# Moving U behind x, zero matmuls ahead of the bands, and a new order of rounds 0 to 5 in a convolution and low-rank mixer kernel

## Chip, cores and metric

The kernel runs on one NeuronCore of a Trainium2 chip. The metric is the device time of one execution in microseconds (us). Before the change three runs gave 346.92, 348.03 and 348.5 us, median 348.03. One more execution was profiled: it took 345.57 us, and the program's own instructions span 343.8 us of it.

## What is computed

Inputs are x (8, 4224, 192), a small weight (8 heads, 7 taps), U (4224, 32), V (32, 4224), w_ch1 (192, 768) and w_ch2 (768, 192), all float32.

```python
w = softmax(weight)                    # 8 heads x 7 taps
y[b,s] = sum_k w[h,k] * x[b, s-6+k]    # causal convolution along s, by head of 24 channels
h = y^T @ U @ V                        # low-rank mixing along s, per batch element
u = y + h^T
out = u + relu(u @ w_ch1) @ w_ch2
```

## The kernel before

The sequence of each of the 8 batch elements is cut into 33 tiles of 128 rows; the 264 tiles of all batches form 33 groups of 8. The order of all work is written out by hand; every engine works its list strictly in that order.

**Start.** From the weight the kernel builds band matrices: softmax of the taps (L219 to L239, VectorE and ScalarE), a turn of the taps on TensorE (L246), seven small matmuls (L254), a product with a mask (L263) and copies into `band_sb` (L280 to L283). `keep_busy` (L213) puts matmuls of the identity, 512 columns each, ahead of and between these steps. Batch 0 is convolved by `conv_whole` (L402): each of four head pairs of each of five blocks of tiles (`blocks_0`) takes four matmuls with 128-row bands, and its result goes from PSUM to `y_sb` by ScalarE (L416) or VectorE (L418) in turn. U is loaded in float32 as 33 rows by the queues of ScalarE and SyncE (L112, L113) and turned on TensorE in four parts of 8 transposes (`turn_U`, L196): two ahead of the convolution, one behind each of its first two blocks. x goes in by GpSimd's queue (L88), cast to bf16 on the way; behind batch 0's five blocks stand V (L336), the halves of w_ch1 (L342), w_ch2 (L348) and batch 1 on that queue.

**Halo.** The convolution reaches six rows back into the tile before. Batch 0 does that with a second matmul. For later batches, `conv_parts` convolves only within the tile, and the first six rows of all tiles are made apart: `load_halo` (L101) loads the rows at the seams, `halo_parts` (steps `h` and `H`) multiplies them with `halo_band`, ScalarE evicts them (L477), one DMA writes them to DRAM (`hy_dr`, L487), and `put_halo` (step `s`, L493) reads them back into `y_sb`. Both DMAs are on SyncE's queue (SP).

**Rounds.** Round g = 0 to 32 does, for group g, the six chunks of the first channel matmul and relu (`m0` to `m5`, L645, evicted by ScalarE at L655 or VectorE at L657), and for group g-1 the second channel matmul in two halves (`P0`/`Q0`, `P1`/`Q1`, 24 matmuls each letter, L377), whose sum with u is formed by VectorE (L664) and written out by SP (L671). It also prepares group g+2: `x0`, `x1` form u (matmul L540, VectorE adds L552 and L560), and `t` turns it by a DMA on SP (L627) into `uT_sb`, which `m0` of round g+2 needs. `y0`, `y1` do the same for one more group. `T` is a turn on TensorE (L611, evicted at L619 and L620), `u` a turn of group 4 by DMA. `cN`/`dN` are the first and second half of a convolution unit; a batch has 8 units. `L` (`low_rank`, L506) is the product with U over all 33 tiles of a batch; its result, evicted by VectorE (L520, L523), is needed by every `x` or `y` step on tiles of that batch. Its first tile has no halo row from the DMA; the other 32 wait for `put_halo`.

Steps in two halves (`Halves`, L377) work on different 64-row parts of the same bank, so the second half waits for a GpSimd nop (L389) that waits for the first half. That nop stands on GpSimd's queue behind whatever loads the list puts there. PSUM has three rotating buffers `big` and one `ch`.

The lists of the rounds around the change, before:

```python
USUAL = "x0 m0 m1 P0 c0 m2 d0 c1 l0 Q0 d1 m3 s m4 L x1 t P1 m5 h Q1 H"
ORDERS = {
    0: "m0 y0 m1 y1 m2 m3 T m4 x0 m5 x1 t b",
    1: "m0 y0 m1 P0 c0 m2 d0 c1 Q0 d1 x0 m3 h m4 H y1 P1 c2 m5 d2 x1 t c3 c4 Q1 d3 d4",
    2: "m0 m1 P0 c0 m2 d0 c1 Q0 d1 m3 c2 m4 d2 s l0 P1 c3 m5 Q1 d3 L",
```

Functions that the diff touches:

Of the kernel before, what the change touches and what calls it, by code (L numbers as in the profile page):

```python
# [11 lines left out]
F32 = mybir.dt.float32  # L12
# [3 lines left out]
def kernel(  # L16
# [53 lines left out]
    def big(dtype=F32, pool=None):  # L70
        return (pool or big_ps).tile([P, 2, BK * 4 // mybir.dt.size(dtype)], dtype, name="big")
# [3 lines left out]

    x_tiles, hx_tiles, hx_bufs = {}, {}, []
    blocks_0 = [(0, 8), (8, 16), (16, 24), (24, 30), (30, NT)]
    assert blocks_0[0][1] >= GT
# [3 lines left out]
    def new_x(b):  # L82
        x_tiles[b] = xs.tile([P, NT + 1, D], BF16, name="x_sb")
        if b < 2:
            nc.vector.memset(x_tiles[b][:, 0, :].bitcast(mybir.dt.uint32), 0)
# [7 lines left out]
    def load_halo(b, s0=0, s1=HS):  # L93

        if s0 == 0 and b < 3:
            hx_bufs.append(cst.tile([P, HS, D], BF16, name=f"hx_sb{b % 2}"))
            nc.vector.memset(hx_bufs[-1][HJ * HP :, :, :], 0.0)
        hx = hx_bufs[(b - 1) % 2]
        for s in range(s0, s1):
            src = x[b, (s + 1) * P - HALO, :]  # L100
            nc.gpsimd.dma_start(  # L101
                out=hx[0 : HJ * HP, s, :],
                in_=bass.AP(src.tensor, src.offset, [[D, HP], [HS * P * D, HJ], [1, D]]),
            )
        hx_tiles[b] = hx

    w_sb = cst.tile([H, KC], F32, name="w_sb")
    nc.sync.dma_start(out=w_sb[:], in_=weight[:])

    U_rows = cst.tile([NT, P * R], F32, name="U_rows")  # L110
    U_dram = moe_U[:].rearrange("(j p) r -> j (p r)", p=P)
    nc.scalar.dma_start(out=U_rows[:, 0 : HB * R], in_=U_dram[:, 0 : HB * R])  # L112
    nc.sync.dma_start(out=U_rows[:, HB * R :], in_=U_dram[:, HB * R :])  # L113
    new_x(0)
# [10 lines left out]
    NA = -(-SP // KC)  # L125
    NCB = -(-(Q + HALO) // KC)
    ident = cst.tile([P, P], BF16, name="ident")
    nc.vector.memset(ident[:].bitcast(U32), 0)
# [37 lines left out]

    at_tap = cst.tile([KC, KC, NQ, Q], BF16, name="at_tap")
    load_x(0, *blocks_0[1])
    for s in blocks_0[2:]:
        load_x(0, *s)  # L170
# [8 lines left out]
    idle_ps = big(pool=ch_ps)  # L179
    ident_ap = ident[:]  # L180
    ident_4 = bass.AP(
        ident_ap.tensor, ident_ap.offset, [list(ident_ap.ap[0]), [0, BK // P], [1, P]]
    )


    ident_32 = cst.tile([NT, NT], F32, name="ident_32")
    nc.vector.tensor_copy(out=ident_32[:], in_=ident[0:NT, 0:NT])
    U_sb = cst.tile([P, R, NT], BF16, name="U_sb")
    UR = R // 4
    assert UR * NT <= BK  # L190

    def turn_U(n):

        ups = big()
        for r in range(UR):
            nc.tensor.transpose(  # L196
                out=ups[:, 0, r * NT : (r + 1) * NT],
                in_=U_rows[:].rearrange("j (p r) -> j r p", r=R)[:, n * UR + r, :],
                identity=ident_32[:],
            )  # L200
        return ups

    def evict_U(n, ups):
        src = ups[:, 0, 0 : UR * NT]
        dst = U_sb[:, n * UR : (n + 1) * UR, :].rearrange("p r j -> p (r j)")
        if n % 2 == 0:
            nc.scalar.activation(out=dst, in_=src, func=ACT.Copy)  # L207
        else:
            nc.vector.tensor_copy(out=dst, in_=src)

    def keep_busy(n):
        for _ in range(n):
            nc.tensor.matmul(  # L213
                out=idle_ps[:, 0, :], lhsT=ident[:], rhs=ident_4, start=True, stop=True
            )
# [12 lines left out]
    )  # L228
    nc.scalar.activation(
        out=halo_band[:].rearrange("p h c -> p (h c)"),  # L230
        in_=ident[:, 0:1].to_broadcast([P, H * P]),
        func=ACT.Copy,
        scale=0.0,
    )
    nc.vector.tensor_scalar_add(s_sb[:], s_sb[:], 1e-9)
# [5 lines left out]
    )  # L241
    for q in range(1, NQ):
        nc.vector.tensor_copy(out=in_band[q * Q : (q + 1) * Q], in_=in_band[0:Q])
    keep_busy(2)
    taps_ps = big(BF16)
    nc.tensor.transpose(out=taps_ps[0:KC, 0, 0:H], in_=tapsT[:], identity=ident[0:H, 0:H])  # L246
    taps = cst.tile([KC, H], BF16, name="taps")
    nc.vector.tensor_copy(out=taps[:], in_=taps_ps[0:KC, 0, 0:H])
    keep_busy(1)


    cps = big()
    for c in range(KC):
# [6 lines left out]
        )  # L260
    U_turned = [turn_U(0), turn_U(1)]
    local = cst.tile([P, H, NA * KC], BF16, name="local")
# [21 lines left out]

    for n, ups in enumerate(U_turned):
        evict_U(n, ups)

# [43 lines left out]

    def load_others():

        def load_V(c0, c1, quads):
            for q in range(quads):
                nc.gpsimd.dma_start(out=V_sb[q * R : (q + 1) * R, c0:c1], in_=moe_V[:, c0:c1])  # L336
            if quads < P // R:
                nc.sync.dma_start(out=V_sb[HB:, c0:c1], in_=V_sb[0:HB, c0:c1])

        load_V(0, V1, P // R)  # L340
        for h in range(2):
            nc.gpsimd.dma_start(  # L342
                out=W1_sb[h * HB : (h + 1) * HB],
                in_=moe_w_ch1[:].rearrange("(k r) m -> r k m", r=HB),
            )
        load_V(V1, 2 * V1, P // R)
        load_V(2 * V1, S, HB // R)
        nc.gpsimd.dma_start(out=W2_sb[:], in_=moe_w_ch2[:].rearrange("(m p) d -> p m d", p=P))  # L348
        new_x(1)
        for s in blocks:  # L350
            load_x(1, *s)

# [370 lines left out]
    for n, (s0, s1) in enumerate(blocks_0):  # L723
        for hh in range(0, H, 2):
            conv_whole(0, s0, s1, hh, hh // 2 % 2, ch_ps if n_conv % 4 == 3 else big_ps)
            n_conv += 1
        if n < 2:
            evict_U(2 + n, turn_U(2 + n))
        if n == 0:
            load_others()  # L730
            halo_masks()
    for s0, s1 in blocks_0:
        low_rank(0, s0, s1)
    straight_mix(0, [straight(0, k) for k in range(KB)])
    load_halo(1)
    new_x(2)
    for s in blocks:
        load_x(2, *s)
    load_halo(2)

    USUAL = "x0 m0 m1 P0 c0 m2 d0 c1 l0 Q0 d1 m3 s m4 L x1 t P1 m5 h Q1 H"
    ORDERS = {
        0: "m0 y0 m1 y1 m2 m3 T m4 x0 m5 x1 t b",
        1: "m0 y0 m1 P0 c0 m2 d0 c1 Q0 d1 x0 m3 h m4 H y1 P1 c2 m5 d2 x1 t c3 c4 Q1 d3 d4",
        2: "m0 m1 P0 c0 m2 d0 c1 Q0 d1 m3 c2 m4 d2 s l0 P1 c3 m5 Q1 d3 L",
        3: "m0 y0 m1 y1 u P0 c0 m2 d0 c1 l0 Q0 d1 x0 m3 m4 x1 t P1 c2 m5 d2 c3 h Q1 H d3",
        4: "x0 m0 m1 P0 c0 m2 d0 c1 l0 Q0 d1 m3 m4 x1 t P1 c2 m5 d2 s Q1",
        5: "x0 m0 m1 P0 c0 m2 d0 c1 l0 Q0 d1 m3 m4 x1 t P1 m5 h Q1 H L",  # L750
        NG - 1: "m0 m1 P0 m2 Q0 m3 m4 m5 W",
    }
    units = [(s0, s1, hh) for s0, s1 in blocks for hh in range(0, H, 2)]
    conv_by = {g: [] for g in range(NG)}
    steps = {g: {} for g in range(NG)}
    for nb in range(1, B):
        last = (nb * NT) // GT - AHEAD - 1
        if nb == 1:
            last, shares = 2, {1: 5, 2: 3}
        elif nb == 2:  # L760
            shares = {2: 1, 3: 4, 4: 3}
        else:
            shares = {g: 2 for g in range(last - 4, last)}
        left = list(units)
# [4 lines left out]
        assert not left  # L769
        at = 3 if nb == 2 else min(shares)  # L770
        steps[at]["h"], steps[at]["H"] = halo_parts(nb)
        steps[max(shares)]["s"] = lambda nb=nb: put_halo(nb)
        steps[last]["L"] = lambda nb=nb: low_rank(nb, 0, NT)
        if nb + 2 < B:


            b, g = nb + 2, max(shares) + (nb > 1)
            for n in range(2):
                steps[g + n]["l0"] = lambda b=b, n=n: (
                    new_x(b) if n == 0 else None,  # L780
                    load_x(b, *blocks[n]),
                )
            steps[g + 2]["l0"] = lambda b=b: load_halo(b)
    for g in range(NG):
# [3 lines left out]
        for m in range(MC):  # L788
            on_act = m not in ((2, 4, 5) if len(conv_by[g]) > 2 and g > 1 else (2, 4))
            if g == 0:  # L790
                on_act = m != 4
            by[f"m{m}"] = lambda g=g, m=m, on_act=on_act: h1_chunk(g, m, on_act)
# [6 lines left out]
        if g != 2 and g + AHEAD < NG:  # L799
            for n in range(2):  # L800
                by[f"x{n}"] = lambda g=g, n=n: mix_quad(g + AHEAD, n * QT)
            by["t"] = lambda g=g: turn_by_dma(g + AHEAD)
        more = {0: 1, 1: 0, 3: 4}
        if g in more:
            for n in range(2):
                by[f"y{n}"] = lambda g=g, n=n: mix_quad(more[g], n * QT)
    steps[0]["T"] = lambda: turn(1, True)
    steps[3]["u"] = lambda: turn_by_dma(4)
    steps[0]["b"] = build_halo_band
    for g in range(NG):  # L810
# [38 lines left out]
```

## Time and profile before

| what | value |
|---|---|
| median of 3 runs | 348.03 us |
| profiled execution | 345.57 us, span 343.8 us, mean granted TensorE clock 0.997 |
| TensorE (PE) busy | 324.3 us, 94% of the span |
| VectorE (DVE), ScalarE (ACT) busy | 229.9 us (67%), 190.4 us (55%) |
| GpSimd (POOL) busy | 48.6 us |
| chain that ended last | PE 70%, DMA 6%, DVE 2% |
| m chunks, L645 | 1188 matmuls, 153.5 us busy |
| W2 and convolution halves, L377 | 3024 matmuls with W_sb, 146.9 us; 224 with band_sb, 34.3 us |
| convolution of batch 0, L402 | 80 matmuls, 10.9 us |

A line of the profile's timeline has start, duration, engine, line, operation, output<-inputs, shape, count, and in brackets the idle time before it with what ended it. Busy times of matmuls overlap, since a matmul is counted until its modelled end; for a pace the starts of neighbouring groups are compared. A table of windows gives busy time of each engine in each stretch, the granted TensorE clock (PEclk), the DMA engines' share and GB/s.

### The profile page before, as it was taken

How to read it: one execution, taken by the hardware profiler on the slowest of the kernel's cores; microseconds unless marked ns; L12 is line 12 of the kernel's file. 1: busy time of each engine (PE TensorE's matmuls, PEld its weight loads, DVE VectorE, ACT ScalarE, POOL GpSimd, SP SyncE). 2: the span in 40 equal slices, each digit the busy share in tenths (PEclk: the TensorE clock that was granted, in tenths of full speed). 3: DMA queues.
4: the chain of work that ended last, by engine and by line, in shares of the span. 5: the costliest groups of instructions: out<-in, count | busy, mean ns of one | idle time of the engine just before them, and what ended most of it. 6: DMA issues, size and time to landing. Idle time of an engine off the chain costs nothing.

```text
span 343.8 us, 11906 instructions
## 1 busy us (share of the span) xinstructions
PE 324.3 (94%) x5319; PEld 243.3 (71%) x5319; DVE 229.9 (67%) x334; ACT 190.4 (55%) x222; POOL 48.6 (14%) x77
## 2 busy tenths in 40 slices
PE   4988888989999999989999999999999999999994
PEld 2874665667677777767777777777777777777774
DVE  5358646957676676657666786667666777777553
ACT  5247564565566656656566665665766444444550
POOL 8485101111012011201012011200000000000000
PEclk9999999999999999999999999999999999999998
DMA  8999997997999669995999699976444644455524
GB/s 129 197 175 193 183 206 119 173 205 165 139 176 236 158 119 210 169 210 148 161 206 236 111 165 193 221 179 143 115 129 136 148 141 139 145 158 157 144 94 139
DMA packets 124064, 56.48 MB, mean 164 GB/s; under 512 B 89008, under 2 KB 123520, under 8 KB 123904
## 3 DMA queue, kind: packets, MB, share of 16 engines
q1 hardware_dynamic: 84160, 39.73, 49.0%
q0 software_dynamic: 39808, 15.70, 39.8%
q8 instruction: 42, 0.69, 0.9%
q10 hardware_dynamic: 44, 0.27, 0.3%
q14 instruction: 10, 0.08, 0.1%
HBM read 32.45 MB, written 26.47 MB: 171 GB/s over the span
## 4 chain that ended last, share of the span: by engine, by line
PE 70%; DMA 6%; DVE 2%; issue 0%; ACT 0%; ACTq 0%
PE big L377 34%; PE big L645 30%; DMA uT_sb<-u_sb 6%; PE big L540 2%; PE big L712 2%; PE big L506 2%; DVE o_sb L664 2%; DVE tt_sb L523 0%; DVE tf_sb L520 0%; ACT hy_sb L477 0%; ACTq L655 0%
## 5 line engine op out<-in xcount | busy, mean ns | idle before, releaser
L655 ACT ACTIVATE rl_sb<-big 128x1024 bf16<-128x1024 f32 x130 | 129.4, 1022 | 87.1 <-PE big L645 84.6
L645 PE MATMUL big<-uT_sb,W_sb 64*128 64x512 bf16 x1188 | 153.5, 376 | 4.3 <-DMA uT_sb<-u_sb 1.4
L377 PE MATMUL big<-W_sb,rl_sb 64*128 64x192 bf16 x3024 | 146.9, 243 | 0.0
L377 PEld LDWEIGHTS <-rl_sb 64*128 64x128 bf16 x3024 | 130.6, 94 | 16.3 <-issue 0.2
L657 DVE TENSOR_SCALAR rl_sb<-big 128x1024 bf16<-128x1024 f32 x68 | 83.3, 1225 | 67.3 <-PE big L645 66.2
L645 PEld LDWEIGHTS <-W_sb 64*128 64x128 bf16 x1188 | 62.7, 94 | 45.3 <-issue 6.2
L664 DVE TENSOR_TENSOR o_sb<-big,u_sb 128x768 f32<-128x768 f32 (+1 forms) x68 | 63.4, 933 | 25.8 <-PE big L377 21.1
L416 ACT ACTIVATE y_sb<-big 128x816 bf16<-128x816 f32 (+4 forms) x66 | 50.7, 771 | 46.1 <-PE big L377 37.3
L552 DVE TENSOR_TENSOR u_sb<-y_sb,big 128x384 bf16<-128x384 bf16 x128 | 64.7, 547 | 1.2 <-PE big L540 1.0
L88 POOL DMA_DIRECT2D x_sb<-in_x_dram x19 | 21.9, 1158 | 118.5 <-PE big L377 117.1
L377 PE MATMUL big<-x_sb,band_sb 64*128 64x408 bf16 (+1 forms) x224 | 34.3, 328 | 1.3 <-ACT rl_sb L655 0.7
L540 PE MATMUL big<-tt_sb,V_sb 64*128 64x192 bf16 x264 | 23.3, 243 | 1.5 <-DVE tt_sb L523 1.0
L101 POOL DMA_DIRECT2D hx_sb<-in_x_dram x28 | 16.0, 578 | 47.0 <-PE big L377 41.9
L540 PEld LDWEIGHTS <-V_sb 64*128 64x128 bf16 x264 | 13.0, 94 | 9.9 <-issue 2.1
L377 PEld LDWEIGHTS <-band_sb 64*128 64x128 bf16 x224 | 12.8, 94 | 7.7 <-issue 1.5
L402 PE MATMUL big<-x_sb,band_sb 128*128 128x192 bf16 (+2 forms) x80 | 10.9, 328 | 0.9 <-DMA x_sb<-in_x_dram 0.9
L402 PEld LDWEIGHTS <-band_sb 128*128 128x128 bf16 x80 | 9.6, 142 | 1.5 <-ACT U_sb L207 1.0
L418 DVE CAST y_sb<-big 128x384 bf16<-128x384 f32 (+2 forms) x10 | 4.8, 488 | 6.8 <-PE big L402 6.8
L506 PEld LDWEIGHTS <-U_sb 128*32 128x32 bf16 x264 | 6.3, 138 | 3.8 <-issue 3.6
L506 PE MATMUL big<-y_sb,U_sb 128*32 128x192 bf16 x264 | 7.8, 252 | 1.2 <-DMA y_sb<-hy_dr 0.8
L477 ACT ACTIVATE hy_sb<-big 48x384 bf16<-48x384 f32 x14 | 6.0, 478 | 4.1 <-PE big L377 4.1
L712 PE MATMUL big<-W_sb,rl_sb 128*128 128x192 bf16 x72 | 6.3, 246 | 1.0 <-DVE o_sb L664 1.0
(66 smaller groups left out, 68.1 us busy)
## 6 DMA issues: line engine op xcount, KB each, us to landing
out_dram<-o_sb SPq DMA_DIRECT2D x65, 384.0 KB, 6.1
x_sb<-in_x_dram POOLq DMA_DIRECT2D x7, 816.0 KB, 11.1
x_sb<-in_x_dram POOLq DMA_DIRECT2D x7, 768.0 KB, 11.4
x_sb<-in_x_dram POOLq DMA_DIRECT2D x3, 384.0 KB, 7.6
hx_sb<-in_x_dram POOLq DMA_DIRECT2D x28, 36.0 KB, 5.8
W_sb<-in_moe_w_ch_dram POOLq DMA_DIRECT2D x3, 288.0 KB, 6.4
V_sb<-in_moe_V_dram POOLq DMA_DIRECT2D x8, 64.0 KB, 6.6
hy_dr<-hy_sb SPq DMA_DIRECT2D x7, 72.0 KB
```

The lines of the kernel that those rows point to most:

```text
L88: nc.gpsimd.dma_start(out=x_tiles[b][:, 1 + s0 : 1 + s1, :], in_=x[b, s0 * P : s1 * P, :].rearrange("(j p) d -> p j d", p=P),)
L101: nc.gpsimd.dma_start(out=hx[0 : HJ * HP, s, :], in_=bass.AP(src.tensor, src.offset, [[D, HP], [HS * P * D, HJ], [1, D]]),)
L377: mm = nc.tensor.matmul(out=out_, lhsT=lhsT[rows], rhs=rhs[rows], start=not second and n == 0, stop=bool(second) and n == N - 1,)
L402: nc.tensor.matmul(out=cps[:, q, 0:n], lhsT=band_sb[:, hh + q, w, :], rhs=x_tiles[b][:, 1 + s0 - w : 1 + s1 - w, hc], start=(w == 0), stop ...
L416: nc.scalar.activation(out=dst, in_=src, func=ACT.Copy)
L506: nc.tensor.matmul(out=tps[q * R : (q + 1) * R, 0, 0:D], lhsT=U_sb[:, :, j], rhs=y_sb[:, j, :], start=(j < n), stop=(j >= NT - n),)
L540: nc.tensor.matmul(out=ups[:, t, i * D : (i + 1) * D], lhsT=V_sb[rows, j * P : (j + 1) * P], rhs=tt_tiles[b][rows, :], start=True, stop=True,)
L552: nc.vector.tensor_tensor(out=dst, in0=y_tiles[b][:, j : j + 2, :].rearrange("p t (k r) -> p t k r", r=HB), in1=add, op=ALU.add,)
L645: nc.tensor.matmul(out=h1[:, q, :], lhsT=W1_sb[rows, k, m * P : (m + 1) * P], rhs=ut[rows, k, :, :], start=(k == 0), stop=(k == KB - 1),)
L655: nc.scalar.activation(out=rl, in_=src, func=ACT.Relu)
L657: nc.vector.tensor_scalar_max(out=rl, in0=src, scalar1=0.0)
L664: nc.vector.tensor_tensor(out=o_sb[:, 0:w, :].rearrange("p t (k r) -> p t k r", r=HB), in0=ch.rearrange("p t (k r) -> p t k r", r=HB), in1 ...
```

## The change

U is loaded in bf16 by GpSimd's queue, behind the second block of x, and turned in two parts of 16 transposes behind the second block of the convolution. Batch 0 has four blocks (8, 11, 9, 5 tiles) in place of five. The matmuls of `keep_busy` take a tile of zeros, which VectorE clears first, in place of the identity that GpSimd makes, and there are 8 + 1 + 5 of them in place of 2 + 1. V goes in by four loads for each column block, with no copy by SP; w_ch1 goes in by halves of its columns; batch 1's two halves, the halo masks and batch 1's halo rows follow on GpSimd's queue. The last block's part of batch 0's low-rank product comes behind the two straight turns of group 0. Group 2 is turned on TensorE in round 1 in place of a DMA in round 0. Batch 1 is convolved in rounds 1 and 2 by 4 + 4 units (5 + 3 before), batch 2 in rounds 3 and 4 by 4 + 4 (1 + 4 + 3 in rounds 2 to 4 before). Batch 1's halo steps `h`, `H` go from round 1 to round 2, and its `L` from the end of round 2 to round 3, behind `m0`. Later loads of x stand at the start of a round.

```diff
-    blocks_0 = [(0, 8), (8, 16), (16, 24), (24, 30), (30, NT)]
+    blocks_0 = [(0, 8), (8, 19), (19, 28), (28, NT)]
...
-    U_rows = cst.tile([NT, P * R], F32, name="U_rows")
-    nc.scalar.dma_start(out=U_rows[:, 0 : HB * R], in_=U_dram[:, 0 : HB * R])
-    nc.sync.dma_start(out=U_rows[:, HB * R :], in_=U_dram[:, HB * R :])
...
+    idle_sb = cst.tile([P, BK], BF16, name="idle_sb")
+    nc.vector.memset(idle_sb[:].bitcast(U32), 0)
...
+    U_rows = cst.tile([NT, P * R], BF16, name="U_rows")
     load_x(0, *blocks_0[1])
+    for c in (slice(0, HB * R), slice(HB * R, P * R)):
+        nc.gpsimd.dma_start(out=U_rows[:, c], in_=U_dram[:, c])
...
-                out=idle_ps[:, 0, :], lhsT=ident[:], rhs=ident_4, start=True, stop=True
+                out=idle_ps[:, 0, :], lhsT=idle_sb[:, 0:P], rhs=idle_sb[:], start=True, stop=True
...
-    for q in range(1, NQ):
-        nc.vector.tensor_copy(out=in_band[q * Q : (q + 1) * Q], in_=in_band[0:Q])
-    keep_busy(2)
+    keep_busy(8)
...
-    U_turned = [turn_U(0), turn_U(1)]
+    keep_busy(5)
...
+    load_V(0, V1)
+    load_W1(slice(0, M4 // 2))
+    load_V(V1, 2 * V1)
+    load_W1(slice(M4 // 2, M4))
+    load_V(2 * V1, 3 * V1)
+    nc.gpsimd.dma_start(out=W2_sb[:], in_=moe_w_ch2[:].rearrange("(m p) d -> p m d", p=P))
+    new_x(1)
+    load_x(1, *blocks[0])
+    load_V(3 * V1, S)
+    load_x(1, *blocks[1])
+    halo_masks()
+    load_halo(1)
...
-        if n < 2:
-            evict_U(2 + n, turn_U(2 + n))
-        if n == 0:
-            load_others()
-            halo_masks()
-    for s0, s1 in blocks_0:
+        if n == 1:
+            turn_U(0)
+            turn_U(1)
+    for s0, s1 in blocks_0[:-1]:
         low_rank(0, s0, s1)
-    straight_mix(0, [straight(0, k) for k in range(KB)])
-    load_halo(1)
-    new_x(2)
-    for s in blocks:
-        load_x(2, *s)
-    load_halo(2)
+    yts = [straight(0, k) for k in range(KB)]
+    low_rank(0, *blocks_0[-1])
+    straight_mix(0, yts)
...
+    USUAL = "l x0 m0 m1 P0 c0 m2 d0 c1 Q0 d1 m3 s m4 L x1 t P1 m5 h Q1 H"
     ORDERS = {
+        0: "m0 m1 y0 m2 y1 m3 T m4 x0 m5 x1",
+        1: "l m0 m1 m2 T y0 P0 c0 m3 d0 c1 Q0 d1 c2 c3 d2 d3 y1 P1 x0 m4 m5 x1 t Q1 b",
+        2: "l m0 m1 c0 P0 c1 d0 c2 d1 Q0 d2 m2 c3 h d3 P1 H m3 s m4 m5 Q1",
+        3: "l m0 L c0 P0 y0 d0 c1 Q0 y1 u d1 m1 m2 m3 x0 P1 c2 c3 d2 x1 t d3 Q1 m4 m5",
+        4: "l c0 c1 d0 d1 m0 P0 c2 c3 d2 d3 x0 Q0 m1 h m2 H P1 m3 s m4 m5 x1 t Q1",
+        5: "l x0 m0 m1 P0 c0 m2 d0 c1 Q0 d1 m3 m4 x1 t P1 L m5 Q1",
...
+    loads = {
+        1: lambda: (new_x(2), load_x(2, *blocks[0])),
+        2: lambda: (load_x(2, *blocks[1]), load_halo(2)),
+        3: lambda: (new_x(3), load_x(3, *blocks[0])),
+        4: lambda: load_x(3, *blocks[1]),
+        5: lambda: load_halo(3),
+    }
...
+    for g in range(2):
+        steps[g]["T"] = lambda g=g: turn(g + 1, True)
```

## Prediction

> **What bounds the kernel now.** First the table of windows, by stage (columns: busy us of PE, PEld, DVE, ACT, POOL, then PEclk, DMA share, GB/s):
>
> ```profile
> 0.00:25.00 25.00, 19.35 (x188) 16.01 (x189) 12.15 (x37) 10.20 (x21) 17.42 (x36) 1.00 1.17 167
> 25.00:57.00 32.00, 28.18 (x403) 18.03 (x401) 20.42 (x31) 20.32 (x25) 8.67 (x12) 1.00 1.26 178
> 57.00:93.00 36.00, 32.70 (x571) 24.16 (x572) 26.06 (x39) 19.38 (x24) 4.77 (x6) 1.00 1.06 167
> 93.00:320.00 227.00, 225.05 (x3887) 170.05 (x3885) 160.57 (x218) 132.89 (x147) 17.77 (x23) 1.00 0.84 165
> ```
>
> From 93 us on TensorE is full: 2 us idle in 227. There every step has a fixed price, read from the starts of neighbouring groups: an m chunk 0.648 us, a P or Q 0.99, a unit's half 0.162 or 0.172, an x, y, h or H 0.165, L 0.86. The change alters almost nothing there; what it can win lies ahead of 93 us. Charging each step its price, TensorE waits 6.6 us between 24.8 us (round 0) and `L` of batch 1 (56.55), 1.1 at that `L`, and 4.3 from there to 92.5.
>
> Then the timeline of TensorE at the start, and the end for comparison:
>
> ```profile
> 8.99 2.72 PE L402 MATMUL big<-x_sb,band_sb 128*128 128x192 bf16 x16 [0.89 <-DMA x_sb<-in_x_dram]
> 11.64 1.09 PE L196 MATMUL big<-ident,U_rows 33*128 33x33 f32 x8
> 12.67 2.74 PE L402 MATMUL big<-x_sb,band_sb 128*128 128x192 bf16 x16
> 15.34 1.09 PE L196 MATMUL big<-ident,U_rows 33*128 33x33 f32 x8
> 16.37 5.45 PE L402 MATMUL big<-x_sb,band_sb 128*128 128x192 bf16 x48
> ...
> 335.91 4.12 PE L712 MATMUL big<-W_sb,rl_sb 128*128 128x192 bf16 x48 [1.05 <-DVE o_sb L664]
> ```
>
> The last 48 of batch 0 stream 16 x (192+144+72) = 6528 columns in 5.45 us, 1.2 a ns; L712 streams 9216 in 4.12, 2.2 a ns. So the convolution of batch 0 ran at half the clock, though the windows print 1.00: the trace has no clock record ahead of 21.19 us, and at that moment the spacing of 72-column matmuls falls from 60 to 33 ns. Half clock cost about 5 us.
>
> Last, what the clock does when TensorE rests, behind the last matmul (ended 340.03):
>
> ```profile
> 340.10:342.00 1.90, 0.00 (x0) 0.00 (x0) 0.32 (x1) 0.00 (x0) 0.00 (x0) 1.00 1.06 354
> 342.10:343.70 1.60, 0.00 (x0) 0.00 (x0) 0.00 (x0) 0.00 (x0) 0.00 (x0) 0.50 0.09 29
> ```
>
> It falls to half 2 us after the last matmul. The two changes of clock, 21.19 and 342.04, lie 94 x 3.413 us apart; so I take windows of about 3.4 us: one 41% busy closed the clock, and those cut by turns of U (66 to 70% convolution) did not open it.
>
> **Part 1, the start.** Before, x landed at 8.86, 11.01, 13.06, 14.67 and 15.43 (the waits of GpSimd's later loads show it): 1200 KB in 6.57 us, 183 KB a us. TensorE at half clock was slower than that, at twice the pace x is. U's 528 KB leave the first microseconds: the first block's packets came 2.6 us after issue where a later load's (54.59) took 2; I take 8.4. Then 528 KB of x, to 11.3; U, 264 KB at the 205 a us of V's loads, to 12.6; 432 KB, to 15.0; 240 KB, to 16.3. Zero matmuls: they start at 1.4, behind a clear of 0.2 us, where the identity kept them until 2.84; eight at 0.427 us (512 columns at 1.2 a ns) last until 4.8, 0.2 past `tapsT` (4.63); the taps copy now stands ahead of 0.98 us of `in_band` copies, and the bands are done at 7.6 as before, under x's 8.4. With the five more TensorE works from 1.4 to at most 7.7, long enough for a whole window nearly always, so I take the full clock. The last block then needs 16 x 55 ns, until 17.3, where before it ended at 21.8. Its eviction (0.7, as `low_rank` shares that PSUM tile), `low_rank` 0.76, two straight turns 0.72, the last `low_rank` 0.14, copy of `part` 0.56, `straight_mix` and its eviction 1.4: first m chunk at 21.6, before 24.8. **-3.2 us.** At half clock throughout: 11.3 + 3.5 + U's turns 1.4 + 2.9 + 1.6 = 20.7, **-0.5**. If x came at 205 a us and U beside it, -4.2.
>
> **Part 2, rounds 0 to 2 and m0 of round 3.** Work: round 0 six m, four x or y, a turn of 12 x 56 ns: 5.2. Round 1 six m, four P or Q, eight unit halves, four x or y, the added turn 0.67, b: 10.7. Round 2 six m, four P or Q, eight halves, h, H: 9.5. Then m0: 0.65. Sum 26.1, against 25.2 before to its `L`. Waits: with three buffers, evictions of 0.97 (ACT m), 1.23 (DVE m), 1.0 (DVE add of an x step), 0.8 (unit), I went through the lists in order and get 4.3 against 6.6: DVE has no 0.8 of halo clears and 0.55 of `halo_band` in round 0, ACT's five m and a turn set its length. TensorE reaches `L` at 21.6 + 26.1 + 4.3 = 52.0; before, 56.55.
>
> Costed at nothing: V's 16 loads and w_ch1's four halves (about 0.5 us of GpSimd each) push batch 1's first half from 30.85 to 31-33; c0 is at 34.8. Without that cover GpSimd's nops queue behind two halo issues and one load of x (0.58+0.58+1.25), up to 2.4. The DMA turn of group 2 (384 KB, 12 us to land) is gone; nobody waited for it.
>
> **Part 3, the wait at L.** Here I see the price. Before, batch 1's halo left ScalarE at 42.3 and `L` came 14 us later; now only m3, m4, m5, Q1 and m0 lie between `H` and `L`: 3 x 0.648 + 0.99 + 0.65 = 3.6 us. The route is long (SP's timeline, then TensorE's):
>
> ```profile
> 42.32 0.33 SPq L487 DMA_DIRECT2D hy_dr<-hy_sb  x1
> 54.52 0.29 SPq L493 DMA_DIRECT2D y_sb<-hy_dr  x1
> ...
> 56.55 0.29 PE L506 MATMUL big<-y_sb,U_sb 128*32 128x192 bf16 x1
> 57.63 0.89 PE L506 MATMUL big<-y_sb,U_sb 128*32 128x192 bf16 x32 [0.79 <-DMA y_sb<-hy_dr]
> ```
>
> Before, SP held the read back until batch 1's last eviction (54.5), so the first leg was covered. By the landing marks, `hy_dr` takes 7.8, 6.1, 6.1, 7.4, 6.7, 6.3 us where x is loading and SP's queue has transfers ahead of it, and 2.55 for the seventh, alone; the read back 3.1 to 5.7. New: H ends at 48.4, eviction 0.2 + 0.86 plus backlog, issue at 49.7. Ahead of it in SP's queue stand group 3's turn (about 41.6) and two outputs, beside x of batch 2 until about 50, then batch 3's first half: landing at 54.9, inside the loaded rows' range less a little; read back 3.3: `L` goes on at 58.2, 6.2 us after it was reached (bounds 55.3 and 63). Everything on TensorE stands behind it: c0, P0, y0; DVE and ACT run dry; SP's outputs stand behind the read back.
>
> 6.2 us contain a whole window, so the clock closes. Half clock until the first full window, 3.4 to 6.8 us, mean 4.5: half is lost, 2.2, less 0.5 of waits on evictions that vanish: +1.7 (bounds 0 and 3.4).
>
> A rule against this change: the Trainium skill (TensorE: Matmul & The Clock Gate, Why this matters for your kernels) asks for no TensorE gap over about 3 us. The rows above price it: half clock for one to two windows, 1.7 to 3.4, so a sum of -0.2 to +1.5.
>
> **Part 4, behind L.** The work left is before's less m0 (0.65), plus one unit of batch 2 (0.34): -0.3. Waits: 4.3 before (0.6 for `tt`, 1.0 and 0.4 at h and H of round 3, 0.8 for group 4's uT, 1.3 at L of batch 2). Now `tt` has c0 and P0 over it, batch 2's `L` has m5 and Q1, group 4's uT lands 4.2 to 8 after issue with 5.6 of work over it: I take 2.1. Gain -2.2.
>
> From round 6 on the order is before's with h one round later and loads moved; two rounds (17 us) remain between H and `L`. Taken as 0, bounds -1 to +1 (one uT wait of 1.4 at 147 us may go or come).
>
> **Sum.** `L` goes on at 58.2 against 57.63: +0.6; clock +1.7; behind -0.3 - 2.2: -0.2 us. 345.57 - 0.2 = 345.4 in the profiled frame (1.8 of it around the span). The median is 2.46 higher: **347.8 us, no change that can be measured** (this kernel's runs tell 0.5%, 1.7 us, from none).
>
> **Rivals.**
> (a) *The halo's route is short.* If SP's queue is empty when `hy_dr` is issued: 2.55 + 3.07, `L` goes on at 55.3, 3.3 us late; the clock closes about half the time (+0.8). -2.3 + 0.8 - 2.5 = -4.0: **344.0**. For it: uncontended rows exist, and group 2's turn is gone from the queue. Against: x of batches 2 and 3 loads just then. 0.35.
> (b) *The zero matmuls don't hold the clock* (the change doesn't do what it says; slower). They open it too late, or the waits for x (8.4, then 9.8 to 11.3, each leaving a window about half busy) close it again. Then the start gains 0.5, not 3.2, and all behind moves by 2.7: -0.2 + 2.7: **350.5**. It decides if a window about half busy closes the gate: one 41% busy did, one 82% busy (21.2 to 24.6) did not. 0.2. By the Trainium skill (TensorE: Matmul & The Clock Gate, Part 1) only a wholly idle window closes it, and (b) would fall; the row at 342 us, where the window still had 1.4 us of matmuls, speaks against that, so (b) stays.
> (c) *The route is longest*: 7.8 + 3.8, `L` at 61.3, and the clock stays half for two windows: +3.7 + 3.4 - 2.5 = +4.6: **352.6**. 0.1.
> Forecast 0.35.
>
> **Numbers.** The forecast's own range: a start of -4.2 and the steady rounds' -1 give 345.8, the clock's 3.4 gives 349.5. The range of 8 in 10 takes in (a) and (b) with their bounds: 341.5 to 352.5. Faster by over 0.5%: (a), 0.35; within: 0.35; slower: (b) and (c), 0.3.
>
> **What would show it.** Spacing of L402's 192-column matmuls, 82 ns (160 in (b)); first m chunk at 21.6; L402's waits for x_sb; a wait of L506 on `y_sb` of 6 us near 52 with granted clock 0.50 behind it; no wait over 1 us at c0 of round 1. I'm wrong if L506 doesn't wait, or if GpSimd's nops wait behind its loads.

## The result and the profile after

| | before | after |
|---|---|---|
| median, 20 runs each, us | 346.0 (343.02 to 350.83) | 350.75 (347.9 to 353.12) |
| ratio of the times | | 1.0148, 95% 1.0114 to 1.0182 |
| profiled execution, span, us | 345.57, 343.8 | 353.12, 351.4 |
| mean granted clock of the profiled execution | 0.997 | 0.973 |

The change makes the kernel 1.5% slower, 5.1 us, where -0.2 us was forecast. That 350.75 lies inside the stated range of 341.5 to 352.5 is luck: the prediction started from a median of 348.03, which over 20 runs is 346.0, and 1.0148 times 348.03 is 353.2, outside. The profiled execution of after is the slowest of its 20: nine of them had a granted clock of 0.973 to 0.979 and took 350.03 to 353.12 us, five had 0.985 to 0.989 and took 347.9 to 350.66.

Line numbers are those of each run's own kernel, so a step's line differs from that of before. The table of windows of after, by the same stages (busy us of PE, PEld, DVE, ACT, POOL; PEclk; DMA share; GB/s):

```profile
0.00:24.80 24.80, 19.16 (x183) 12.89 (x184) 11.44 (x35) 9.64 (x18) 17.77 (x34) 0.86 1.04 135
24.80:56.30 31.50, 29.06 (x417) 18.76 (x417) 19.93 (x29) 21.97 (x26) 13.23 (x24) 1.00 1.36 174
56.30:63.80 7.50, 0.50 (x11) 0.34 (x13) 0.06 (x1) 1.02 (x1) 0.00 (x0) 0.69 1.27 215
63.80:69.30 5.50, 5.50 (x80) 4.51 (x74) 2.14 (x6) 0.85 (x1) 0.00 (x0) 0.50 0.00 0
```

The start takes as long as before, 24.8 us. Its clock of 0.86 can't be set against the 1.00 of before, whose trace has no record ahead of 21.19 us. Then come a hole of 7 us and 5.5 us at half clock behind it. TensorE's timeline of after, at the start and at the hole:

```profile
7.24 1.78 PE L398 MATMUL big<-x_sb,band_sb 128*128 128x192 bf16 x16 [0.59 <-ACT band_sb L268]
11.42 3.57 PE L398 MATMUL big<-x_sb,band_sb 128*128 128x264 bf16 x16 [2.40 <-DMA x_sb<-in_x_dram]
14.93 2.19 PE L191 MATMUL big<-ident,U_rows 33*128 33x33 bf16 x32
17.05 3.67 PE L398 MATMUL big<-x_sb,band_sb 128*128 128x216 bf16 x32
...
24.77 0.39 PE L641 MATMUL big<-uT_sb,W_sb 64*128 64x512 bf16 x2 [0.26 <-ACT uT_sb L596]
...
56.28 0.29 PE L502 MATMUL big<-y_sb,U_sb 128*32 128x192 bf16 x1
63.57 1.51 PE L502 MATMUL big<-y_sb,U_sb 128*32 128x192 bf16 x32 [7.00 <-DMA y_sb<-hy_dr]
```

The first 16 matmuls of L398 ran at full clock (1.78 us for 16 x 192 columns), the next 16, at 11.42, at half (3.57 us for 16 x 264, 1.2 columns a ns). Why shows in windows laid on the clock's changes, which fall 3.41 us apart:

```profile
4.50:7.90 3.40, 2.70 (x21) 1.21 (x20) 2.70 (x10) 1.56 (x3) 3.40 (x6) 1.00 1.43 161
7.90:11.30 3.40, 1.12 (x14) 0.89 (x11) 1.19 (x3) 1.35 (x3) 1.21 (x3) 1.00 1.31 169
11.32:14.72 3.40, 3.30 (x16) 2.25 (x16) 1.15 (x2) 0.61 (x1) 1.74 (x3) 0.50 1.50 186
14.73:18.13 3.40, 3.40 (x46) 3.18 (x45) 1.20 (x3) 1.35 (x3) 1.51 (x4) 1.00 1.16 180
18.15:21.50 3.35, 2.89 (x32) 2.64 (x33) 1.52 (x4) 1.66 (x4) 3.35 (x7) 0.50 0.96 133
```

A window 33% busy (the wait for x) is followed by one at half clock. The one from 14.73 is full by the table, but 2.19 us of it are the turns of U (L191); it too is followed by half clock. So windows less than about half full close the gate, which is rival (b)'s mechanism, and turns don't fill them, which is in none of the rivals. The Trainium skill (TensorE: Matmul & The Clock Gate, Part 1) puts the fall to half rate behind a window of idleness; the window here was 33% busy and one of e11, shown below, 40%, so the measured share decides. By the Trainium skill (TensorE: Matmul & The Clock Gate, Part 4: PE-mode transpose) transposes don't count as busy in the same way; the window from 14.73 agrees.

SP's timeline of after has the halo's route:

```profile
45.23 4.13 SPq L623 DMA_TRANSPOSE uT_sb<-u_sb  x1
49.41 1.99 SPq L667 DMA_DIRECT2D out_dram<-o_sb  x2
53.35 0.57 SPq L483 DMA_DIRECT2D hy_dr<-hy_sb  x1
58.56 0.32 SPq L489 DMA_DIRECT2D y_sb<-hy_dr  x1
```

The write to DRAM landed at 58.54, right behind the two outs queued ahead of it (56.94 and 58.35); the read back took until 63.53. A load of x, half of batch 3, was in flight beside both (issued at 52.94, landed at 63.32).

### The profile page after: what moved, and what is told of

The parts are those of the page before. It is cut to its first block, busy times and chain, and to the rows that moved or that the text cites. A ratio compares the mean times of both kernels' runs of the same rounds, so it can differ in the third digit from the quotient of the medians.

```text
span 351.4 us, 11913 instructions
## 1 busy us (share of the span) xinstructions
PE 327.6 (93%) x5326; PEld 239.2 (68%) x5326; DVE 224.5 (64%) x327; ACT 194.5 (55%) x224; POOL 53.4 (15%) x86
## 4 chain that ended last, share of the span: by engine, by line
PE 75%; DMA 16%; DVE 3%; ACT 2%; issue 1%; POOL 0%; POOLq 0%; ACTq 0%
PE big L373 35%; PE big L641 30%; DMA uT_sb<-u_sb 11%; PE big L536 2%; PE big L502 2%; DMA x_sb<-in_x_dram 2%; PE big L398 2%; PE big L708 2%; DVE o_sb L660 1%; DMA hy_dr<-hy_sb 1%; DMA y_sb<-hy_dr 1%; ACT rl_sb L651 1%; ACT y_sb L412 1%; PE big L191 1%; DVE u_sb L548 1%
## 5 line engine op out<-in xcount | busy, mean ns | idle before, releaser
L651 ACT ACTIVATE rl_sb<-big 128x1024 bf16<-128x1024 f32 x134 | 133.6, 1022 | 88.8 <-PE big L641 87.6
L641 PE MATMUL big<-uT_sb,W_sb 64*128 64x512 bf16 x1188 | 151.4, 376 | 4.9 <-DMA uT_sb<-u_sb 1.8
L653 DVE TENSOR_SCALAR rl_sb<-big 128x1024 bf16<-128x1024 f32 x64 | 78.4, 1225 | 63.0 <-PE big L641 61.7
L641 PEld LDWEIGHTS <-W_sb 64*128 64x128 bf16 x1188 | 59.7, 94 | 49.1 <-issue 8.3
L412 ACT ACTIVATE y_sb<-big 128x816 bf16<-128x816 f32 (+5 forms) x64 | 49.9, 790 | 47.1 <-PE big L373 39.3
L89 POOL DMA_DIRECT2D x_sb<-in_x_dram x18 | 21.6, 1203 | 129.0 <-PE big L641 52.0
L502 PEld LDWEIGHTS <-U_sb 128*32 128x32 bf16 x264 | 7.0, 141 | 10.5 <-issue 10.4
L398 PE MATMUL big<-x_sb,band_sb 128*128 128x192 bf16 (+3 forms) x64 | 8.9, 316 | 3.1 <-DMA x_sb<-in_x_dram 2.4
L398 PEld LDWEIGHTS <-band_sb 128*128 128x128 bf16 x64 | 6.8, 126 | 5.1 <-DMA x_sb<-in_x_dram 2.6
L327 POOL DMA_DIRECT2D V_sb<-in_moe_V_dram x16 | 8.1, 527 | 5.0 <-DMA x_sb<-in_x_dram 5.0
L516 DVE COPY tf_sb<-big 64x192 f32<-64x192 f32 x8 | 2.9, 359 | 9.0 <-PE big L502 8.8
L414 DVE CAST y_sb<-big 128x384 bf16<-128x384 f32 (+3 forms) x8 | 4.6, 570 | 5.6 <-PE big L398 5.4
```

The source lines that it names most:

```text
L89: nc.gpsimd.dma_start(out=x_tiles[b][:, 1 + s0 : 1 + s1, :], in_=x[b, s0 * P : s1 * P, :].rearrange("(j p) d -> p j d", p=P),)
L398: nc.tensor.matmul(out=cps[:, q, 0:n], lhsT=band_sb[:, hh + q, w, :], rhs=x_tiles[b][:, 1 + s0 - w : 1 + s1 - w, hc], start=(w == 0), stop ...
L502: nc.tensor.matmul(out=tps[q * R : (q + 1) * R, 0, 0:D], lhsT=U_sb[:, :, j], rhs=y_sb[:, j, :], start=(j < n), stop=(j >= NT - n),)
L641: nc.tensor.matmul(out=h1[:, q, :], lhsT=W1_sb[rows, k, m * P : (m + 1) * P], rhs=ut[rows, k, :, :], start=(k == 0), stop=(k == KB - 1),)
L651: nc.scalar.activation(out=rl, in_=src, func=ACT.Relu)
L653: nc.vector.tensor_scalar_max(out=rl, in0=src, scalar1=0.0)
```

## The experiments

Theory A: batch 1's halo comes back too late for the earlier `L`; the wait and the half clock behind it eat the gain. Theory B: the start lost it, since the gate closes on the waits for x and on the turns. Rivals: the new order of rounds, or the contention with loads of x, is what costs. A zero matmul is one of `idle_sb`, 512 columns; `hold(n)` issues n of them. Edits are to the changed kernel unless another is named; ratios are to the kernel before.

**e1: no wait for the halo.** Batch 1's halo rows are made and written to DRAM but not added to y.

```diff
-        steps[max(shares)]["s"] = lambda nb=nb: put_halo(nb)
+        if nb > 1: steps[max(shares)]["s"] = lambda nb=nb: put_halo(nb)
```

> The halo rows of batch 1 are not read back into y (the step s of batch 1 is left out), so L has no DMA to wait for; six rows of each tile of batch 1 then lack their halo. Theory A (the loss is the wait at L and the clock that closes in it): the wait of 7.0 us goes, the clock stays at 1.00 from the first rounds on, 5.5 us of half clock behind L go (2.7 us of time). Time 9 to 10 us below the changed kernel, ratio to the kernel before 0.985 to 0.990. Theory B (the loss is at the start, where the clock closed twice; at L the time would come back in other waits, of evictions or of the turns by DMA): 0 to 3 us below, ratio 1.006 to 1.015.

Ratio 0.9879 (0.9829 to 0.9929), 2.7% or 9.3 us below after. TensorE's timeline has no hole:

```profile
55.97 0.96 PE L502 MATMUL big<-y_sb,U_sb 128*32 128x192 bf16 x33
56.87 0.35 PE L373 MATMUL big<-x_sb,band_sb 64*128 64x408 bf16 x2
```

Theory A is shown: without the wait the change beats the kernel before by 4.2 us. The first m came at 24.34 all the same, so the start is a loss of its own. The gain without the wait also answers the rival that the new order of rounds is what costs: on balance it isn't.

**e2 and e11: zero matmuls in the hole,** 33 and 20, between round 3's `m0` and its `L`.

```diff
-        3: "l m0 L c0 P0 ...",
+        3: "l m0 z L c0 P0 ...",
+    steps[3]["z"] = lambda: hold(33)   # e11: hold(20)
```

> 33 matmuls of zeros, 512 columns each (7.1 us at 0.216), stand between m0 and L of round 3, so TensorE works while the halo is on its way. Theory A with the clock as its second half: the wait at L falls to under 1 us, its time is filled and not won, the clock stays open behind L, and 2.7 us are won: ratio about 1.007. If the half clock behind L costs nothing (evictions would bound those steps anyway): ratio 1.015 as before. If zeros don't keep the gate open: clock 0.50 behind L and 1.015.

> The changed kernel with 20 zero matmuls (some 4.3 us at full clock) between the m of round 3 and its L, so that they end before the halo's return lands, while the 33 of the earlier run ran past it. The route of the halo is as it was, the wait at L should fall from 7.0 to about 2.7 us. If the price of the closed clock is the 2.7 us by which the time behind L differs between the changed kernel and the version without the wait, and the filled window stays open, the run is 2.7 us shorter than the changed kernel: ratio 1.005 to 1.008. If the window closes all the same, on the 2.7 us that are left idle, the ratio stays at 1.013 to 1.017.

e2: 1.0104 (1.0048 to 1.0161), between the two expectations. The clock was full behind `L`, from which 279.7 us remained to the last matmul against 283.2 in after, but the zeros ran 2.1 us past the landing: in its profile group 3's turned tile came 2.8 us late ahead of them, and the clock was half from 56.70 to 60.12, while they ran. e11: 1.0065 (1.0023 to 1.0107), the number that the first theory gave, but not its mechanism: the windows of e11 show that the 2 us left idle closed the gate all the same, for one window (three in after).

```profile
53.61:57.01 3.40, 3.35 (x16) 1.54 (x16) 0.00 (x0) 1.02 (x1) 0.00 (x0) 1.00 1.58 205
57.02:60.42 3.40, 1.36 (x15) 0.54 (x17) 0.00 (x0) 0.00 (x0) 0.00 (x0) 1.00 1.02 198
60.43:63.83 3.40, 3.40 (x60) 2.77 (x55) 1.06 (x3) 0.00 (x0) 0.00 (x0) 0.50 0.01 3
```

From `L` on to the last matmul e11 took 282.4 us, 0.8 less than after. Where the rest of its 2.9 us comes from its one profile can't tell: that run's start was also at full clock throughout (first m 21.15).

**e3: the halo a round earlier.** `b`, `h`, `H` in round 1, `s` right behind `d3` in round 2.

```diff
-        1: "... y0 P0 c0 ... y1 P1 x0 m4 m5 x1 t Q1 b",
-        2: "... Q0 d2 m2 c3 h d3 P1 H m3 s m4 m5 Q1",
+        1: "... y0 b P0 c0 ... y1 P1 h x0 m4 H m5 x1 t Q1",
+        2: "... Q0 d2 c3 m2 d3 s P1 m3 m4 m5 Q1",
...
-            last, shares, at = 3, {1: 4, 2: 4}, 2
+            last, shares, at = 3, {1: 4, 2: 4}, 1
```

> The halo steps h and H of batch 1 go into round 1 (its band b ahead of them), and s stands right behind the last unit of round 2. Nothing else moves. Theory A: the write of the halo rows is issued near 43 instead of 53, ahead of group 3's turn in SP's queue, and lands before the last unit is evicted near 52; the read back lands 3 to 5 us later, at 55 to 57, with L reached at 56: wait at L 0 to 1.5 us, clock open behind it, 7 to 10 us below the changed kernel, ratio 0.986 to 0.995. Theory B: 0 to 3 us below. A third way: h waits for its rows (landed 39.3) or its nop behind a load, and round 1 grows by 1 to 3 us: ratio 0.993 to 1.003.

1.0009 (0.9966 to 1.0051), 4.8 us less than after, but above the 0.986 to 0.995 of theory A. SP's timeline and TensorE's show why not all of it:

```profile
42.38 0.35 SPq L483 DMA_DIRECT2D hy_dr<-hy_sb  x1
43.58 3.50 SPq L623 DMA_TRANSPOSE uT_sb<-u_sb  x1
47.13 1.95 SPq L667 DMA_DIRECT2D out_dram<-o_sb  x2
50.17 2.06 SPq L489 DMA_DIRECT2D y_sb<-hy_dr  x1
```

```profile
54.40 0.82 PE L641 MATMUL big<-uT_sb,W_sb 64*128 64x512 bf16 x6 [1.94 <-DMA uT_sb<-u_sb]
55.15 0.30 PE L502 MATMUL big<-y_sb,U_sb 128*32 128x192 bf16 x1
58.84 1.50 PE L502 MATMUL big<-y_sb,U_sb 128*32 128x192 bf16 x32 [3.39 <-DMA y_sb<-hy_dr]
```

The read back is issued 8.4 us earlier than in after (58.56), but behind group 3's turn (landed 54.36) and two outs (to 57.95): 8.6 us, to 58.80. So `m0` and `L` waited 5.3 us in all, and the clock was half from 55.39 to 62.21.

**e9: group 3 turned on TensorE in round 2,** not by DMA; the halo where the change put it. **e6: both,** e3 and this.

```diff
-        1: "... x1 t Q1 b",
-        2: "l m0 m1 c0 ...",
+        1: "... x1 Q1 b",
+        2: "l m0 m1 T c0 ...",   # e6: T behind P1, the halo steps as in e3
...
-            if g > 0: by["t"] = lambda g=g: turn_by_dma(g + AHEAD)
+            if g > 1: by["t"] = lambda g=g: turn_by_dma(g + AHEAD)
...
-    for g in range(2):
+    for g in range(3):
         steps[g]["T"] = lambda g=g: turn(g + 1, True)
```

> The changed kernel with only group 3's turn moved from SP's queue to TensorE, in round 2. The halo steps stay where the change put them. In the changed kernel turn, two outputs, halo write and read back landed at 55.5, 56.9, 58.4, 58.5 and 63.5. If the queue ahead sets the halo's route: the write lands 3 us earlier, the read back too, the wait at L falls from 7.0 to 3 to 5 us, ratio 1.003 to 1.010. If the route has its own length (2.6 us and 3.1 us are the shortest rows, 5 and 5 the ones here): wait 6 to 7 us, ratio 1.013 to 1.017.

> As e3_early_halo (batch 1's h and H in round 1, s behind the last unit), and group 3 is turned on TensorE in round 2 (12 transposes, 0.67 us) in place of the DMA in SP's queue, behind which two outputs and the read back landed one after another in e3 (54.4, 55.5, 58.0, 58.8). If that queue is what is left of the wait: the read back lands 3 to 5 us after its issue near 50, L doesn't wait, m0 of round 3 doesn't wait for its turn (2.1 us in e3), the clock stays open: 5 to 7 us below e3, ratio 0.980 to 0.988. If x loading slows the read back whatever stands in SP's queue: L still waits 2 to 4 us, ratio 0.995 to 1.001.

e9: 1.0143 (1.0082 to 1.0203), no gain. Its write took 1.8 us with the queue empty, but the read back 6.6 (53.82 to 60.40): `L` still waited 5.5. SP's timeline of e9, and TensorE's:

```profile
52.01 0.35 SPq L483 DMA_DIRECT2D hy_dr<-hy_sb  x1
53.82 0.32 SPq L489 DMA_DIRECT2D y_sb<-hy_dr  x1
```

```profile
60.44 1.51 PE L502 MATMUL big<-y_sb,U_sb 128*32 128x192 bf16 x32 [5.54 <-DMA y_sb<-hy_dr]
```

e6: 0.9846 (0.9790 to 0.9902), 5.3 us below the kernel before: the lowest ratio here. SP's timeline of e6, and TensorE's:

```profile
42.78 0.35 SPq L483 DMA_DIRECT2D hy_dr<-hy_sb  x1
44.83 4.23 SPq L667 DMA_DIRECT2D out_dram<-o_sb  x2
50.56 0.33 SPq L489 DMA_DIRECT2D y_sb<-hy_dr  x1
```

```profile
53.82 0.83 PE L641 MATMUL big<-uT_sb,W_sb 64*128 64x512 bf16 x6
54.58 0.96 PE L502 MATMUL big<-y_sb,U_sb 128*32 128x192 bf16 x33
```

The read back landed 3.1 us after issue, ahead of `L`; behind `L` 280.6 us remain. Against after, the early halo alone gives 4.8 us, the turn alone nothing that can be told, both 10.4. Against the kernel before, e6's profile is 2.9 us ahead at the first m (21.88), 3.1 at `L` and 4.9 at the last matmul.

Why e9's read back took twice as long as e6's, nothing in SP's queue says. The landings of x fit the rival of contention. In e6, e8, e10 and e12 the read back was issued 0.04 to 0.08 us ahead of the load of batch 3's first half and took 3.0 to 3.3 us (in e3 as well, but there the turn and two outs stood ahead of it). In after, e2, e4, e7, e9 and e11 it was issued 2.2 to 8.5 us behind that load, took 3.9 to 6.6 us, and landed between 1.2 us ahead of the load and 0.6 behind it. No run moved the load alone, so this cause is argued, not shown.

**e10: e6 with few zeros** (2 + 1 in place of 8 + 1 + 5).

```diff
-    keep_busy(8)
+    keep_busy(2)
-    keep_busy(5)
```

> The version with the early halo steps and group 3 turned on TensorE, with 2 zero matmuls instead of 8 ahead of the bands and none of the 5 behind the casts of x. It asks what the zero matmuls are worth by themselves. If the granted clock at the start is set by how full TensorE is in each window of 3.41 us, the clock opens later, part of the convolution of batch 0 runs at half clock, and the first matmul of m comes at 24 to 25 us instead of 21.9: 2 to 3 us more than the version it comes from, a ratio to the kernel before of 0.990 to 0.994. The rival says that the landings of x set the start: then the first m stays at 21.4 to 22.1 us and the ratio at 0.985.

0.9927 (0.9870 to 0.9983), as the clock theory said; the clock opened at 13.86, the first m came at 23.97 (e6: 21.88), behind `L` the times are equal. So the eleven further zero matmuls are worth 2 to 3 us (2.1 by the two profiles, 2.8 by the ratios, whose intervals just overlap).

**e4, e7, e8: the start held open.** e4: 11 zeros behind block 0 and one behind every fourth turn of U. e7: 8 zeros behind block 0, the two parts of U's turn behind blocks 1 and 2. e8: e6 with e7's edit.

```diff
+        if n == 0: hold(8)               # e4: hold(11)
-        if n == 1: turn_U(0); turn_U(1)
+        if n in (1, 2): turn_U(n - 1)    # e4: turns as they were, a zero after each 4
```

> Matmuls of zeros fill the start: 11 of 512 columns behind the first block of batch 0's convolution (2.4 us, where TensorE waited 2.4 us for x), and one behind every fourth transpose of U (8 in all). Theory B (the start's gain was lost to the clock): the 264-column matmuls take 110 ns instead of 220, the 216-column ones 92 instead of about 130, the first m chunk of round 0 comes at 22 to 23 instead of 24.8, all behind it moves with it: 2 to 3 us below the changed kernel, ratio about 1.007. If x's landing alone sets the start: 0 to 1 us, ratio 1.012 to 1.015. The wait at L stays at 6 to 8 us in both.

> The changed kernel with 8 matmuls of zeros behind the first block of batch 0's convolution (1.7 us, less than the wait for x there) and the two parts of U's turn apart, behind the second and the third block, so that no clock window is filled by turns alone. If the clock is what takes the start's gain in most executions: the clock is closed less often in the first 22 us, the first m chunk comes at 21 to 22.5, 1.5 to 3 us below the changed kernel, ratio 1.006 to 1.011; the wait at L stays 6 to 8 us. If the phase of the windows decides whatever is filled in: no change, 1.015.

> e6 and e7 together: halo of batch 1 early, group 3 turned on TensorE, the start's clock held. If the two losses are separate and add: ratio of e6 less 0.005 to 0.008, so 0.973 to 0.983, below the kernel before. If one covers the other (an earlier start waits longer for x of batch 1, for V or at L): as e6.

e4: 1.0212 (1.0154 to 1.0270), a miss: TensorE's timeline shows each group of four turns drawn out to 0.67 to 0.9 us with its zero, 5.9 us in all in place of 2.2, and the clock closed again.

```profile
15.84 0.43 PE L192 MATMUL big<-ident,U_rows 33*128 33x33 bf16 x4
16.20 0.39 PE L211 MATMUL big<-idle_sb 128*128 128x512 bf16 x1
16.52 0.42 PE L192 MATMUL big<-ident,U_rows 33*128 33x33 bf16 x4
16.88 0.56 PE L211 MATMUL big<-idle_sb 128*128 128x512 bf16 x1
```

e7: 1.0180 (1.0119 to 1.0240); the profile has a held clock from 6.66 to 57.86 and the first m at 22.58, and yet no gain. There the loss lies behind `L`: 289.3 us to the last matmul against 283.2 in after, with waits for turned groups of 6.8 us in all, the longest 3.7 at 119.17, and half clock for a window behind that one. The profiled execution took 357.78 us and the median 353.56, so this doesn't explain the others. e8: 0.9879 (0.9824 to 0.9934), not told from e6. Filling by hand won nothing over e6; what e7 lost is open.

**e12: e6 with group 2 turned by DMA behind round 0,** as before the change.

```diff
-        0: "... x0 m5 x1",
-        1: "l m0 m1 m2 T y0 b ...",
+        0: "... x0 m5 x1 t",
+        1: "l m0 m1 m2 y0 b ...",
...
-            if g > 1: by["t"] = lambda g=g: turn_by_dma(g + AHEAD)
+            if g != 1: by["t"] = lambda g=g: turn_by_dma(g + AHEAD)
```

> The version with the early halo steps and group 3 turned on TensorE, but with group 2 of batch 1 turned by DMA behind round 0, where the changed kernel turns it on TensorE in round 1. It takes about 0.67 us of matmul work out of round 1 (the price of one such turn by the difference between the versions with one and two of them) and puts one DMA transpose into SP's queue ahead of the loads of x and the outs. If nothing in that queue is late for it: ratio 0.982 to 0.984. If the transpose holds up what is queued behind it, or lands too late for round 2's m0, 1 to 3 us slower: ratio 0.988 to 0.994, with a wait for the turned group or for x in rounds 1 to 2.

0.9948 (0.9909 to 0.9986), 3.5 us over e6, just above the slower of the two expectations. The wait is at `h`, for batch 1's halo rows:

```profile
42.75 0.34 PE L373 MATMUL big<-hx_sb,halo_band 64*128 64x96 bf16 x8 [2.31 <-DMA hx_sb<-in_x_dram]
```

The turn, issued at 32.47, landed 9.8 us later; from 37.0 to 41.6 the DMA engines moved 94 to 156 GB/s (e6 at that time: 161 to 210), a load of x took 14.3 us (e6: 10.9), and the wait closed the gate for one window. Of the 4.6 us between the last matmuls of the two profiles, 1.2 are the start, where the gate closed in e12 and not in e6.

**e13: the new start with the old rounds,** the lists of before and x of batch 2 loaded ahead of round 0. (The change also moves some `m` chunks between ScalarE and VectorE, `ON_VECTOR`; they go back too.)

```diff
+    new_x(2)
+    for s in blocks: load_x(2, *s)
+    load_halo(2)
-    ORDERS = {0: "m0 m1 y0 ...", ...}    # the changed lists, shares and loads
+    ORDERS = {0: "m0 y0 m1 ...", ...}    # those of before
```

> The changed kernel's start (U in bf16 behind x and turned late, the zero matmuls, four blocks, the new order of loads) with the lists of rounds of the kernel before: group 2 turned by DMA in round 0, batch 1's halo steps in round 1 and its L at the end of round 2, x of batch 2 loaded ahead of round 0. If the start's gain reaches the end, the run is shorter than before by what the first matmul of m gains, 0.3 to 1.3 us where the clock closes at the start and 2.7 to 3.4 where it holds, and there is no wait over 1.5 us at L: ratio 0.991 to 0.998. The rival says that the old lists give the gain back, because batch 1's x or halo rows then come late for the earlier steps of round 1: a wait of 1 to 3 us for x_sb or hx_sb in round 1 and a ratio of 0.999 or more.

1.0326 (1.0274 to 1.0377): the gain is lost, as the rival said, but far more than that, and in a wait that it didn't name. GpSimd's and TensorE's timelines:

```profile
33.88 2.52 POOL L89 DMA_DIRECT2D x_sb<-in_x_dram  x2
36.36 0.62 POOL L99 DMA_DIRECT2D hx_sb<-in_x_dram  x1
40.25 1.13 POOL L99 DMA_DIRECT2D hx_sb<-in_x_dram  x2 [3.27 <-DMA x_sb<-in_x_dram]
42.03 0.56 POOL L99 DMA_DIRECT2D hx_sb<-in_x_dram  x1 [0.65 <-issue]
```

```profile
42.19 0.86 PE L373 MATMUL big<-x_sb,band_sb 64*128 64x408 bf16 x4 [8.60 <-POOLq L385]
```

`d0` waits 8.6 us for its nop, which stands on GpSimd's queue behind the loads of batch 2. The new start needs the loads at the heads of rounds; what it is worth without that obstacle wasn't measured apart from e10.

## Why the prediction was wrong

The forecast of 347.8 failed at two steps: the start's full clock, which it took as good as sure, and the price of the wait at `L`, which it put too low. The direction of the forecast, no change, was wrong.

**Part 1 failed at "so I take the full clock".** Where the clock held, the first m came at 21.15 to 22.12, forecast 21.6. It held in five of the nine profiles with this unaltered start (e3, e6, e9, e11, e13); in the others (after, e1, e2, e12) it closed and the first m came at 23.0 to 24.8. The windows keep their own time: the first recorded opening lay at 4.19 to 7.07. So the wait for x (1.6 to 2.5 us) and the turns (2.2, forecast 1.4) fall otherwise into the windows from run to run. In the five, every window up to the first m was at least 43% full, turns left out; in the four, the gate closed behind windows of 26 to 40%. The windows of e6:

```profile
7.06:10.46 3.40, 1.96 (x19) 1.38 (x17) 2.01 (x5) 2.29 (x4) 2.04 (x4) 1.00 1.47 189
10.47:13.87 3.40, 2.75 (x29) 2.32 (x30) 1.42 (x2) 1.22 (x2) 1.74 (x3) 1.00 1.45 190
13.88:17.28 3.40, 3.29 (x46) 3.20 (x45) 1.68 (x4) 1.40 (x3) 0.99 (x2) 1.00 1.25 186
```

Here the first window is 58% full where after's was 33%, and the turns (13.06 to 15.22) fall into the second and the third. Two things in Part 1 made the hole deeper than forecast. The first block of x landed at 6.58, not 8.4, while the second came as forecast (11.38 for 11.3), so TensorE waited 2.4 us between them where 1.5 was forecast. And the prediction had itself read that windows cut by turns of U didn't open the gate, but gave 32 turns in a row no price beyond their 1.4 us. I weighed the waits for x as rival (b), 0.2, with 350.5; its condition, that a window about half busy closes the gate, is what the traces show. In after's profile the start cost 3.2 us more than forecast. The -0.5 for a start at half clock doesn't follow from its own terms: 20.7 and the 4.3 us behind the last block make 25.0, 0.2 later than before, so (b) should have stood near 351.2.

**Part 2:** rounds 0 to 2 and `m0` took 31.5 us (24.77 to 56.28), forecast 30.4. The work is the list of steps that was priced (26.1), so the 1.1 are waits: about 5.4 where 4.3 was forecast.

**Part 3:** the mechanism was right and the place too, the price too small. The write took 5.19 us (forecast 5.2), the read back 4.97 (3.3); `L` went on 7.3 us late, forecast 6.2. Half clock lasted from 59.10 to 69.34, 5.77 us of it with work, so by estimate 2.9 were lost where 1.7 was taken. By the runs, after against e1, wait and clock together cost 9.3 us; forecast 7.9.

**Part 4 was about right:** 283.2 us behind `L` less the estimated 2.9 is 280.3, against 282.4 before: -2.1, forecast -2.5. Runs with a full clock behind `L` agree, from 279.0 (e1) to 280.6 (e6, e10): -3.4 to -1.8. For the steady rounds no difference is left over.

In the profile the steps miss by 3.2 + 1.1 + 1.1 + 1.6 = 7.0 us; the last matmul ended at 346.76 for a forecast of 339.8. By the medians the miss is 5.3 (5.1 for -0.2): 1.4 at `L`, and 3.9 elsewhere, since without the wait the forecast would have been -8.1 and e1 measured -4.2. How much of the 3.9 is the start's clock in the runs that weren't profiled stays open. Rival (a) needed a short route: e9 had its short write (1.8 us) and still waited 5.5, since the read back grew. "Nobody waited for it", of group 2's DMA turn, held before, not under the new start: e12 gains nothing from bringing it back, it loses 3.5.

## What to carry to other kernels

When a consumer is moved up, take its slowest supplier with it: here a round trip through DRAM of 6 to 15 us (write and read back of batch 1 together, e13 and e3) needed a round of its own and a DMA queue without a transpose in it, and only both edits together brought the time below that of before. Count a hole in TensorE's work with the half clock behind it, and count windows half empty, turns left out, as holes. An engine's queue that carries both loads and the nops of another engine's steps must be planned anew when the loads move.

## What the runs showed of the hardware

- In 14 profiles (before, after and the 12 experiments) every window of 3.41 us behind which the clock fell was at most 46% busy with matmuls other than turns; windows of 48% and more kept it, and from 43 to 46% it went both ways. A half clock was raised behind windows of 82% and more, not behind those of 75% and less (one of e4's, 83% with zeros between turns, did not raise it). The ends of matmuls are modelled, so these are no sharp thresholds.
- Zero matmuls count as work: in after they opened the clock at 4.49.
- 32 turns of 33 columns took 2.14 to 2.19 us, at half granted clock (e1, 2.18) as at full (e3, e6, after).
- Batch 1's write to DRAM (72 KB) took 1.8 us in e9, where SP's queue was empty and all loads but one, issued 0.4 us before, had landed, and 5.1 to 8.1 in after, e2, e4 and e6, with earlier loads or outs in flight; its read back took 3.0 (e8) to 8.6 us (e3).
